# Block-causal attention and a gated MLP on one core: decode steps of the weights ranked below attention, constants by casting transfers, and two blocks of the weights' product side by side

## The chip, the cores and the metric

One core of one Trainium2 chip. The metric is the device time of one execution in microseconds. Engines are called as the profile calls them: PE (matrix), PEld (its weight loads), DVE (vector), ACT (scalar), POOL (GpSimd), SP (issues transfers only). Each engine takes its instructions in a fixed order, one after the other.

## The reference

```python
# batch 8, heads 8, seq 576, head_dim 64, blocks of 64; d_model 512, d_ff 1024
scores = q @ k.T / sqrt(64)                   # block-causal mask: block_i >= block_j
attn = exp(scores - rowmax); attn = attn / (sum(attn) + 1e-9)
x = concat_heads(attn @ v)                    # 4608 x 512
h = ((x @ w1) * (x @ w2)) @ w3
out = h @ w_out                               # float32
```

## The kernel before, in words

Heads are taken in pairs: a batch has four pairs, and there are 32 in all. `pair(n)` does the two heads j = 0 and 1 of pair n: score tiles s (a PSUM tile of up to 512 columns, two in turn), their exponentials pe, and the products x with the values; ahead of it, for the next pair, a bound on the row maxima from bf16 copies kb and qd (`shift_mask`: products mx, maxima m on DVE, a transposition mt, the negated result ms on ACT), which is written into a row of qk, the operand of the score matmuls (`shift`: for pair 0 by DVE from constants, for the others by POOL copies for pair 1 and small transfers qk<-ms that ACT issues). `prep_qk` rounds q and k into qk and subtracts to get the low parts. `norm` and `finish_x` divide by the row sums and split x into xh (ACT) and xl (POOL).

The MLP of one batch is the work beside the attention of the next. For batch 0 there is none yet, so its four pairs (the early stage, n < EARLY) run beside the preparation of the weights instead:

- The weights come as 64-bit numbers in 40 units of 0.5 MB, and `load_w` decodes one unit: a transfer wraw (five buffers); on ACT `wy` (the high word scaled, three buffers) and `top` (one byte of `wbits`, two of these buffers in turn); on POOL `low` (another byte of `wbits`); on DVE a combine of the two. Eight units are w_out (`wo`), sixteen w3, eight each w1 and w2. Those of w1 and w2 are then split (`load_rows`): a cast to w1h or w2h on DVE and a subtraction to w1l or w2l on POOL.
- `gen_prod` multiplies w3 by w_out on PE into W, eight blocks of eight matmuls, so that the MLP needs one product less. A block is copied out as wh and wl.

The order on PE is the order in which the code is written, for which EARLY_PLAN has one letter for each step of a pair's two heads: S a score tile, M a step of the next pair's maxima, B and A the preparations of q and k (own second head, next pair), V the products with v, Q loads the pair after next, N and T take and normalize x, C decodes one or two units (`weights`), W does two matmuls of W (`prod`). On the other engines the scheduler orders the instructions by rank and by when it expects their inputs; rank is the order of the code unless it is shifted. Each engine then waits in that order.

After pair 3 the rest of W is computed, the early buffers are given up, and the late stage begins, with attention of one batch beside the MLP of the one before.

Of the kernel before, what the change touches and what calls it, by code (L numbers as in the profile page):

```python
# [8 lines left out]
F32 = mybir.dt.float32  # L9
F32R = mybir.dt.float32r  # L10
BF16 = mybir.dt.bfloat16
I32 = mybir.dt.int32
# [36 lines left out]
)  # L49

EARLY_PLAN = (
# [8 lines left out]
)  # L60

DELAY = 3

# [4 lines left out]
def block_causal_attention__then__gated_mlp_kernel(ctx, tc, qkv, consts, ident_in, w1, w2, w3t, wout, out_t):  # L68
# [37 lines left out]
        raw_of[n] = t  # L106

    load(0)
    for t, tag in enumerate(("tr", "x32")):
        cst = work.tile([P, S], F32, tag=tag, name=f"cst{t}")  # L110
        nc.sync.dma_start(out=cst[0:D], in_=consts[:, t * S : (t + 1) * S])
        for j in range(2):
            nc.gpsimd.tensor_copy(qk[j][oth[j], 3 * t, :], cst[0:D])
    nc.sync.dma_start(out=both, in_=ident_in)
    nc.gpsimd.memset(qd, 0.0)

    tl = {}

    def open_early(pool):
        tl["early"] = pool  # L120
        tl["wo"] = pool.tile([P, NF, DM], F32, name="wo")
        tl["bits"] = [pool.tile([P, 512], I32, name=f"wbits{u}") for u in range(2)]
        tl["unit"] = 0
        for t in tl["bits"]:
            nc.gpsimd.memset(t, 0)

    def open_late():
        pool = ctx.enter_context(tc.tile_pool(name="late", bufs=1, reuse_waits="tile"))
# [7 lines left out]
        tl["gl"] = pool.tile([P, NF, HALF], F32R, name="gl")  # L136

    def load_w(dst, src):
        t = tl["early"].tile([P, 1024], I32, tag="wraw", name="wraw", bufs=5)
        y = tl["early"].tile([P, 512], F32, tag="wy", name="wy", bufs=3)  # L140
        bits = tl["bits"][tl["unit"] % 2]
        tl["unit"] += 1
        nc.sync.dma_start(out=t, in_=src)
        high = t.rearrange("p (c two) -> p c two", two=2)[:, :, 1]
        byte = t.bitcast(U8).rearrange("p (c e) -> p c e", e=8)
        if dst is None:
            dst = y
        low = bits.bitcast(U8).rearrange("p (c e) -> p c e", e=4)[:, :, 0]
        top = bits.bitcast(F8).rearrange("p (c e) -> p c e", e=4)[:, :, 3]
        nc.scalar.mul(out=y, in_=high.bitcast(F32), mul=2.0**-112)  # L150
        nc.scalar.activation(out=top, in_=byte[:, :, 7], func=AF.Copy, bias=127.5 * 2.0**-60, scale=-(2.0**-60), saturate=False)  # L151
        nc.gpsimd.tensor_scalar(out=low, in0=byte[:, :, 3], scalar1=1.0 / 32, scalar2=-31.0 / 64, op0=ALU.mult, op1=ALU.add)  # L152
        nc.vector.scalar_tensor_tensor(out=dst.bitcast(I32), in0=y.bitcast(I32), scalar=3, in1=bits, op0=ALU.logical_shift_left, op1=ALU.bitwise_or)
        return y
# [65 lines left out]
    def prep_qk(n, j):  # L220
        rqk = raw_of[n][:, 0 : 2 * S].rearrange("p (t s) -> p t s", t=2)
        o, x = own[j], oth[j]
        if j == 1:
            shift(n, 1)
        cast(n, qk[j][o, 0:2], rqk[o], CAST[0])
        yield
        if n == 0:
            copy = nc.gpsimd.tensor_copy if j else nc.scalar.copy
            copy(qk[j][x, 1, :], rqk[o, 1, :])
            copy(qk[j][x, 2, :], rqk[o, 0, :])  # L230
        else:
            queue(n).dma_start(out=qk[j][x, 1, :].bitcast(F32), in_=qk[j][o, 1, :].bitcast(F32))
            queue(n).dma_start(out=qk[j][x, 2, :].bitcast(F32), in_=qk[j][o, 0, :].bitcast(F32))
        yield
        (nc.gpsimd if "late" in tl or n * j else nc.vector).tensor_tensor(out=qk[j][o, 2:4], in0=rqk[o], in1=qk[j][o, 0:2], op=ALU.subtract)  # L235
        yield

    def prep_v(n, j):
        rv = raw_of[n][:, 2 * S :].rearrange("p (j c d) -> p j c d", j=2, c=5)[:, j]
        if n < EARLY:  # L240
            if n == 0:
                tl["ve", j] = tl["early"].tile([P, 5, P], F32, name=f"ve{j}")
                nc.gpsimd.memset(tl["ve", j][:, :, oth[j]], 1.0)
            nc.scalar.copy(tl["ve", j][:, :, own[j]], rv)
            return
        v = tl["vs"][j]
        cast(n, v[:, :, own[j]], rv, CAST[3])
        nc.gpsimd.tensor_tensor(out=v[:, :, oth[j]], in0=rv, in1=v[:, :, own[j]], op=ALU.subtract)
# [125 lines left out]
    def gen_w(wp):  # L374
        def rows(u):
            for k in range(2 * u, 2 * u + 2):
                load_w(tl["wo"][:, k, :], wout[k])

        def w3(m):
            assert done[0] >= m - 1  # L380
            t3_of[m] = wp.tile([P, NF, P], F32, tag="w3", name="w3", bufs=2)
            for h in range(2):
                load_w(t3_of[m][:, 4 * h : 4 * h + 4, :].rearrange("p k f -> p (k f)"), w3t[2 * m + h])

        def split(dst_h, dst_l, src):
            g = load_rows(dst_h, dst_l, src)
            return lambda _: next(g)

        one, two = split(w1h, w1l, w1), split(w2h, w2l, w2)
        for u in range(4):  # L390
            rows(u)
            yield
        m, rest = 0, [one] * 4 + [two] * 4
        while m < NF or rest:
            if m < NF and done[0] >= m - 1 and (m < 2 or len(rest) <= 9 - m or not rest):
                w3(m)
                m += 1
            else:
                rest.pop(0)(None)
            yield  # L400

    def gen_prod():
        wo = tl["wo"]
        for m in range(NF):
            acc = ps_m.tile([P, 512], F32, tag="psm", name=f"w{m}")
            for k in range(NF):
                nc.tensor.matmul(acc, t3_of[m][:, k, :], wo[:, k, :], start=(k == 0), stop=(k == NF - 1))  # L407
                if k % 2 and k < NF - 1:
                    yield
            nc.scalar.copy(wh[:, m, :], acc)  # L410
            nc.vector.tensor_tensor(out=wl[:, m, :], in0=acc, in1=wh[:, m, :], op=ALU.subtract)
            done[0] += 1
            yield

    def gen_moe(b):
        mp, gh, gl = tl["late"], tl["gh"], tl["gl"]
# [51 lines left out]
    def pair(n):  # L468
# [9 lines left out]
        for j in range(2):  # L478
            xps = ps_x.tile([P, 1024], F32, tag="psx", name=f"x{n}_{j}")
            p_early = wp.tile([P, 1600], F32, tag="pe", name=f"pe{n}_{j}") if early else None  # L480
            tiles = s_tiles(n, j, p_early)
            pvs = (pv_early if early else pv)(n, j, xps, p_early)
            delay = DELAY if n == NPAIR and j == 0 else 0
            for step in (EARLY_PLAN[n] if early else PLAN)[j].split():
                if step in "CW":
                    fill(weights if step == "C" else prod, 1)
                    continue
                with tc.high_priority(offset=0) if early else nullcontext():
                    if step == "S":
                        fill(tiles, 1)  # L490
                    elif step == "F":
                        if delay:
                            delay -= 1
                        else:
                            fill(mlp, 1)
                    elif step == "M":
                        fill(masks, 1)
                    elif step == "A":
                        fill(next_qk, 1)
                    elif step == "B":  # L500
                        fill(own_qk, 1)
                    elif step in "UV":
                        fill(pvs, 1)
                    elif step == "R":
                        sums(n, j, part)
                    elif step == "N" and early:
                        take_early(n, j, xps, x32, rr)
                    elif step == "N":
                        take(n, j, xps, x32)
                    elif step == "T":  # L510
                        if not early:
                            total(n, part, rr)
                        norm(n, x32, rr)
                        finish_x(n, x32)
                    elif step == "Q" and not last:
                        if n + 1 != NPAIR:
                            prep_v(n + 1, j)
                        if j == 1 and n + 2 < NN:
                            load(n + 2)
# [69 lines left out]
```

## Time and profile before

| | |
|---|---|
| median of 3 runs | 980.52 us (980.49 to 980.68) |
| the profiled execution | 982.55 us |
| its span, first to last instruction | 980.6 us |
| busy share of PE, DVE, ACT, POOL | 96%, 71%, 57%, 64% |
| mean granted clock of PE | 0.993 |

The profile lists for each engine when an instruction began, how long it took, and what ended the idle time before it. `[3.81 <-DMA qk<-ms]` behind a row is 3.81 us of idle time of that engine, ended by the landing of that transfer; rows that follow each other are merged, with their count behind an x. PE is the engine to watch: where it is idle, something else sets the pace. Buffer numbers are left out of names.

### The profile page before, as it was taken

The numbers are of one execution on the slowest core, as the hardware profiler recorded it, in microseconds if no ns is written. First come the engines' busy times: TensorE is split into PE (matmuls) and PEld (weight loads), VectorE is DVE, ScalarE is ACT, GpSimd is POOL, SyncE is SP. The second block draws the span as 40 slices with busy tenths as digits, with TensorE's granted clock in tenths as the row PEclk, the third lists the DMA queues.
The fourth block names the chain that finished last, engine by engine and source line by source line (L and its number), as shares of the span: only waits on it lengthen the run. The fifth ranks groups of instructions, "written<-read, shape, count | busy, mean of one in ns | idle before, by whom it ended". The sixth has DMA issues, their size and how long they took to land.

```text
span 980.6 us, 18312 instructions
## 1 busy us (share of the span) xinstructions
PE 941.6 (96%) x6594; PEld 879.1 (90%) x6624; DVE 692.4 (71%) x1230; ACT 557.3 (57%) x1451; POOL 629.6 (64%) x605
## 2 busy tenths in 40 slices
PE   3788989999999999999999999999999999999998
PEld 1444449999999999999999999999999999999998
DVE  6776857777777778878777777788787877774100
ACT  6776635656556665566565556655656555553221
POOL 6786737767676767677676767676776767673211
PEclk9999989999999999999999999999999999999999
DMA  8967502222222221222222221211222222100000
GB/s 294 304 198 221 163 19 62 63 75 63 87 63 75 63 87 41 66 69 65 73 66 83 64 80 57 88 54 53 69 72 66 69 81 63 50 13 25 7 19 25
DMA packets 31303, 79.81 MB, mean 81 GB/s; under 512 B 5356, under 2 KB 13676, under 8 KB 31212
## 3 DMA queue, kind: packets, MB, share of 16 engines
q1 hardware_dynamic: 29788, 76.26, 25.4%
q10 hardware_dynamic: 1424, 2.38, 1.0%
q8 instruction: 52, 0.85, 0.4%
q14 instruction: 39, 0.32, 0.1%
HBM read 50.76 MB, written 9.44 MB: 61 GB/s over the span
## 4 chain that ended last, share of the span: by engine, by line
PE 88%; ACT 3%; DVE 3%; POOL 3%; issue 2%; DMA 1%; ACTq 0%; SPq 0%; POOLq 0%; DVEq 0%
PE ab L426 42%; PE o L442 21%; PE s L265 9%; PE x L320 9%; PE mx L192 3%; PE w L407 2%; POOL wbits L152 1%; ACT wbits L151 1%; DMA wraw<-in_w 1%; ACT wy L150 1%; POOL w2l L162 1%; PE x L304 1%; DVE m L196 1%; ACT pe L273 1%; DVE qk L166 0%
## 5 line engine op out<-in xcount | busy, mean ns | idle before, releaser
L286 POOL TENSOR_TENSOR rsum<-rsum,p 128x448 f32<-128x448 f32 x224 | 186.1, 831 | 87.1 <-ACT p L280 76.8
L435 POOL TENSOR_TENSOR gl<-g,gh 128x288 fp32r<-128x288 f32 x128 | 114.5, 895 | 121.5 <-ACT gh L434 121.5
L283 DVE TENSOR_TENSOR pl<-p,ph 128x448 fp32r<-128x448 f32 x168 | 149.1, 901 | 60.1 <-ACT ph L281 59.2
L265 PE MATMUL s<-qk 128*128 128x288 f32 (+4 forms) x768 | 157.3, 314 | 16.3 <-ACT pe L273 10.8
L235 POOL TENSOR_TENSOR qk<-raw,qk 64x1152 fp32r<-64x1152 f32 x58 | 154.9, 2670 | 9.1 <-issue 6.1
L426 PE MATMUL ab<-xh,w2h 128*128 128x288 f32 x512 | 153.8, 300 | 0.0
L442 PE MATMUL o<-gh,wh 128*128 128x288 f32 x512 | 153.6, 300 | 0.0
L426 PE MATMUL ab<-xh,w1h 128*128 128x288 f32 x512 | 151.1, 295 | 0.0
L426 PE MATMUL ab<-xl,w2h 128*128 128x288 f32 x512 | 151.0, 295 | 0.0
L426 PE MATMUL ab<-xl,w1h 128*128 128x288 f32 x512 | 151.0, 295 | 0.0
L426 PE MATMUL ab<-xh,w1l 128*128 128x288 f32 x512 | 151.0, 295 | 0.0
L442 PE MATMUL o<-gh,wl 128*128 128x288 f32 x512 | 150.9, 295 | 0.0
L426 PE MATMUL ab<-xh,w2l 128*128 128x288 f32 x512 | 150.9, 295 | 0.0
L442 PE MATMUL o<-gl,wh 128*128 128x288 f32 x512 | 150.8, 295 | 0.0
L265 PEld LDWEIGHTS s<-qk 128*128 128x128 f32 (+1 forms) x768 | 116.9, 183 | 28.5 <-ACT pe L273 16.1
L434 ACT CAST gh<-g 128x288 fp32r<-128x288 f32 x128 | 55.4, 433 | 142.8 <-DVE g L433 142.7
L281 ACT ACTIVATE ph<-s 128x288 fp32r<-128x288 f32 x336 | 131.4, 393 | 0.0
L196 DVE TENSOR_REDUCE m<-mx 128x1 f32<-128x64 f32 (+3 forms) x320 | 128.3, 446 | 3.0 <-PE mx L192 0.8
L280 ACT ACTIVATE p<-s 128x448 f32<-128x448 f32 x224 | 85.5, 382 | 51.5 <-PE s L265 50.7
L283 DVE TENSOR_TENSOR pl<-rsum,ph 128x288 fp32r<-128x288 f32 x112 | 75.7, 677 | 49.2 <-ACT ph L281 45.4
L320 PE MATMUL x<-ph,vs 128*128 128x128 f32 x336 | 110.4, 329 | 0.0
L433 DVE TENSOR_TENSOR g<-ab,a 128x288 f32<-128x288 f32 x128 | 56.5, 441 | 69.5 <-PE ab L426 68.6
(76 smaller groups left out, 2182.4 us busy)
## 6 DMA issues: line engine op xcount, KB each, us to landing
raw<-in_qkv SPq DMA_DIRECT2D x31, 896.0 KB
qk<-qk SPq DMA_DIRECT2D x108, 144.0 KB
out_t<-o SPq DMA_DIRECT2D x64, 144.0 KB
wraw<-in_w3t SPq DMA_DIRECT2D x16, 512.0 KB
wraw<-in_w SPq DMA_DIRECT2D x16, 512.0 KB
wraw<-in_wout SPq DMA_DIRECT2D x8, 512.0 KB
qk<-qk ACTq DMA_DIRECT2D x16, 144.0 KB
qk<-ms SPq DMA_DIRECT2D x54, 2.2 KB
```

Source lines behind the costliest of these rows:

```text
L196: nc.vector.reduce_max(m[:, col : col + 1], sc, axis=AX.X)
L235: (nc.gpsimd if "late" in tl or n * j else nc.vector).tensor_tensor(out=qk[j][o, 2:4], in0=rqk[o], in1=qk[j][o, 0:2], op=ALU.subtract)
L265: nc.tensor.matmul(t[ks, at : at + q1 - q0], qk[j][:, k, kr], qk[j][:, q, q0:q1], start=(s == 0), stop=(s == 1))
L280: nc.scalar.activation(p32, t[ks, at : at + w], AF.Exp, scale=SCALE)
L281: nc.scalar.activation(ph[ks, o : o + w], t[ks, at : at + w], AF.Exp, scale=SCALE)
L283: nc.vector.tensor_tensor(out=low, in0=p32, in1=ph[ks, o : o + w], op=ALU.subtract)
L286: nc.gpsimd.tensor_tensor(out=r, in0=r, in1=p32, op=ALU.add)
L320: nc.tensor.matmul(xps[:, to : to + w], v[:, c, :], pr[:, a : a + w], start=(u < 2 and s == 0), stop=(u in (0, len(PV) - 1) and s == len(p ...
L426: nc.tensor.matmul(t[:, 0:HALF], l[:, c, fs], r, start=(c == 0 and s == 0), stop=(c == NC - 1 and s == 2))
L433: nc.vector.tensor_tensor(out=g32, in0=acc[1][:, 0:HALF], in1=a32, op=ALU.mult)
L435: nc.gpsimd.tensor_tensor(out=gl[:, f, :], in0=g32, in1=gh[:, f, :], op=ALU.subtract)
L442: nc.tensor.matmul(t[:, 0:HALF], l[:, f, es], r[:, f, :], start=(f == 0 and s == 0), stop=(f == NF - 1 and s == 2))
```

## The change

Six edits, all of the early stage.

1. Ranks: the steps C rank as if they stood 400 places later in the code. Before, attention steps had a shift of 0, decode steps none. The order of PE stays that of the code.
2. Constants: two transfers issued by POOL write them, cast, into qk; before, SP loaded them into two tiles and POOL cast them in four copies. The memsets at the start move from POOL to DVE.
3. `top` of the first twelve units moves from ACT to POOL (a comparison and a product that give the same byte).
4. Pair 0's two subtractions in `prep_qk` move from DVE to POOL.
5. Blocks 0 and 1 of W run side by side, one matmul of each in turn, so the order of the weights is w3's first two blocks, then w_out, then the rest. w3 gets three buffers instead of two, wraw four instead of five. W's steps C and W are placed anew in EARLY_PLAN.
6. A block of w3 may be decoded two blocks ahead of the product instead of one.

```diff
-    ("B B C M S S W B M S S M W C S M W V V M V V V Q N",
-     "M S S A C W S M S A W C S W V V A M V V V Q N T W W"),
+    ("B B C M S S W B M S S W M W C S M W V V M V V V Q N",
+     "M S S A C W S M S A C S W V V A M V W V V Q N T W W W W W"),
...
+LATER = 400
...
-    for t, tag in enumerate(("tr", "x32")):
-        cst = work.tile([P, S], F32, tag=tag, name=f"cst{t}")
-        nc.sync.dma_start(out=cst[0:D], in_=consts[:, t * S : (t + 1) * S])
-        for j in range(2):
-            nc.gpsimd.tensor_copy(qk[j][oth[j], 3 * t, :], cst[0:D])
+    for j in range(2):
+        nc.gpsimd.dma_start(out=qk[j][oth[j], 0:4:3, :], in_=consts.rearrange("p (t s) -> p t s", t=2))
     nc.sync.dma_start(out=both, in_=ident_in)
-    nc.gpsimd.memset(qd, 0.0)
+    nc.vector.memset(qd, 0.0)
...
-        t = tl["early"].tile([P, 1024], I32, tag="wraw", name="wraw", bufs=5)
+        t = tl["early"].tile([P, 1024], I32, tag="wraw", name="wraw", bufs=4)
...
-        nc.scalar.activation(out=top, in_=byte[:, :, 7], func=AF.Copy, bias=127.5 * 2.0**-60, scale=-(2.0**-60), saturate=False)
+        if tl["unit"] <= 12:
+            top = bits.bitcast(U8).rearrange("p (c e) -> p c e", e=4)[:, :, 3]
+            nc.gpsimd.tensor_scalar(out=top, in0=byte[:, :, 7], scalar1=128.0, scalar2=128.0, op0=ALU.is_ge, op1=ALU.mult)
+        else:
+            nc.scalar.activation(out=top, in_=byte[:, :, 7], func=AF.Copy, bias=127.5 * 2.0**-60, scale=-(2.0**-60), saturate=False)
...
-        (nc.gpsimd if "late" in tl or n * j else nc.vector).tensor_tensor(out=qk[j][o, 2:4], in0=rqk[o], in1=qk[j][o, 0:2], op=ALU.subtract)
+        (nc.gpsimd if "late" in tl or n == 0 or j else nc.vector).tensor_tensor(out=qk[j][o, 2:4], in0=rqk[o], in1=qk[j][o, 0:2], op=ALU.subtract)
...
-            assert done[0] >= m - 1
-            t3_of[m] = wp.tile([P, NF, P], F32, tag="w3", name="w3", bufs=2)
+            assert done[0] >= m - 2
+            t3_of[m] = wp.tile([P, NF, P], F32, tag="w3", name="w3", bufs=3)
...
+        for m in range(2):
+            w3(m)
+            yield
         for u in range(4):
             rows(u)
             yield
...
-            if m < NF and done[0] >= m - 1 and (m < 2 or len(rest) <= 9 - m or not rest):
+            if m < NF and done[0] >= m - 2:
...
+        acc = [ps_m.tile([P, 512], F32, tag="psm", name=f"w{m}") for m in range(2)]
+        for k in range(NF):
+            for m in range(2):
+                part(acc[m], m, k)
+            if k == NF - 1:
+                for m in range(2):
+                    out(acc[m], m)
             yield
...
                 if step in "CW":
-                    fill(weights if step == "C" else prod, 1)
+                    with tc.high_priority(offset=-LATER) if step == "C" else nullcontext():
+                        fill(weights if step == "C" else prod, 1)
                     continue
-                with tc.high_priority(offset=0) if early else nullcontext():
+                with nullcontext():
```

How this moves instructions is seen at three places. Numbers behind names tell tiles apart; they differ between the two kernels, and lines L are those of each kernel's own code (POOL's L152 is `low` before, `top` after; after, `low` is L155).

POOL between the shift copy of pair 1's second head and pair 0's product x, before:

```order
L216 COPY qk_87<-qk_87 9x576
L152 TENSOR_SCALAR wbits_109<-wraw 128x512
L235 TENSOR_TENSOR qk_87<-raw_188,qk_87 64x1152
L152 TENSOR_SCALAR wbits_110<-wraw 128x512
L358 TENSOR_TENSOR x_0_190<-x_0_190,rb_372 128x576
```

and after (six rows of three more units, which read like those ahead, are left out at the mark):

```order
L219 COPY qk_87<-qk_87 9x576
L152 TENSOR_SCALAR wbits_104<-wraw 128x512
L155 TENSOR_SCALAR wbits_104<-wraw 128x512
L238 TENSOR_TENSOR qk_87<-raw_184,qk_87 64x1152
L152 TENSOR_SCALAR wbits_103<-wraw 128x512
L155 TENSOR_SCALAR wbits_103<-wraw 128x512
...
L155 TENSOR_SCALAR wbits_103<-wraw 128x512
L361 TENSOR_TENSOR x_0_186<-x_0_186,rb_372 128x576
```

Two wbits steps became eleven (the one before x belongs to the thirteenth unit, whose `top` is on ACT again).

ACT at the same time, from pair 0's xh to pair 1's first exponentials, before:

```order
L367 CAST xh_0_375<-x_0_190 128x288
L367 CAST xh_1_379<-x_0_190 128x288
L151 ACTIVATE wbits_109<-wraw 128x512
L150 ACTIVATE wy<-wraw 128x512
L151 ACTIVATE wbits_110<-wraw 128x512
L166 CAST qd<-raw_365 64x9x64
L273 ACTIVATE pe_0_391<-s_0_423 128x288
L273 ACTIVATE pe_0_391<-s_0_419 128x288
```

and after:

```order
L370 CAST xh_0_375<-x_0_186 128x288
L370 CAST xh_1_379<-x_0_186 128x288
L276 ACTIVATE pe_0_386<-s_0_396 128x288
L276 ACTIVATE pe_0_386<-s_0_400 128x288
L149 ACTIVATE wy<-wraw 128x512 x2
```

The decode steps and the cast qd went from between xh and the exponentials; xh still stands ahead of them.

ACT ahead of the second head's first exponentials of pair 2, before:

```order
L273 ACTIVATE pe_0_634<-s_0_707 64x64
L151 ACTIVATE wbits_109<-wraw 128x512
L151 ACTIVATE wbits_110<-wraw 128x512
L150 ACTIVATE wy<-wraw 128x512 x2
L232 DMA qk_86<-qk_86 64x576
L233 DMA qk_86<-qk_86 64x576
L151 ACTIVATE wbits_109<-wraw 128x512
L244 COPY ve_154<-raw_606 128x5x64
L150 ACTIVATE wy<-wraw 128x512
L273 ACTIVATE pe_1_738<-s_1_744 128x288
```

and after:

```order
L276 ACTIVATE pe_0_605<-s_0_680 64x64
L154 ACTIVATE wbits_103<-wraw 128x512
L149 ACTIVATE wy<-wraw 128x512
L154 ACTIVATE wbits_104<-wraw 128x512
...
L149 ACTIVATE wy<-wraw 128x512
L247 COPY ve_148<-raw_584 128x5x64
L154 ACTIVATE wbits_103<-wraw 128x512
L349 COPY x_2_602<-x_0_604 64x576
L276 ACTIVATE pe_1_731<-s_1_737 128x288
```

Six decode steps stood between the two heads' exponentials, and nine stand there now (some left out here).

From the first `ab` matmul, the first exponentials ph and the first output transfer on, every engine has the same rows as before.

More of the change, by code (lines that the diff above doesn't have):

```diff
@@ L124, in open_early @@
         for t in tl["bits"]:
-            nc.gpsimd.memset(t, 0)
+            nc.vector.memset(t, 0)
     def open_late():
@@ L242, in prep_v @@
                 tl["ve", j] = tl["early"].tile([P, 5, P], F32, name=f"ve{j}")
-                nc.gpsimd.memset(tl["ve", j][:, :, oth[j]], 1.0)
+                nc.vector.memset(tl["ve", j][:, :, oth[j]], 1.0)
             nc.scalar.copy(tl["ve", j][:, :, own[j]], rv)
@@ L392, in gen_w @@
             yield
-        m, rest = 0, [one] * 4 + [two] * 4
+        m, rest = 2, [one] * 4 + [two] * 4
         while m < NF or rest:
-            if m < NF and done[0] >= m - 1 and (m < 2 or len(rest) <= 9 - m or not rest):
+            if m < NF and done[0] >= m - 2:
                 w3(m)
@@ L398, in gen_w @@
             else:
-                rest.pop(0)(None)
+                what = rest.pop(0)
+                what(None)
             yield
@@ L403, in gen_prod, with part, out @@
         wo = tl["wo"]
[L404 to L409, printed above, removed]
+        def part(acc, m, k):
+            nc.tensor.matmul(acc, t3_of[m][:, k, :], wo[:, k, :], start=(k == 0), stop=(k == NF - 1))
+        def out(acc, m):
             nc.scalar.copy(wh[:, m, :], acc)
@@ L412, in gen_prod @@
             done[0] += 1
-            yield
+        acc = [ps_m.tile([P, 512], F32, tag="psm", name=f"w{m}") for m in range(2)]
[5 more added lines that the diff above has]
+                    out(acc[m], m)
+            yield
+        for m in range(2, NF):
+            acc = ps_m.tile([P, 512], F32, tag="psm", name=f"w{m}")
+            for k in range(NF):
+                part(acc, m, k)
+                if k == NF - 1:
+                    out(acc, m)
+                if k % 2:
+                    yield
     def gen_moe(b):
```

12 rows, old and new, of the table EARLY_PLAN are left out of this document.

## The prediction

> **What bounds the kernel now.** I read the page's busy shares and its 40 slices first, then busy time by stage, then the PE timeline of the slices that are not full.
>
> ```profile
> PE 941.6 (96%) x6594; PEld 879.1 (90%) x6624; DVE 692.4 (71%) x1230; ACT 557.3 (57%) x1451; POOL 629.6 (64%) x605
> PE   3788989999999999999999999999999999999998
> PEclk9999989999999999999999999999999999999999
> ```
>
> PE is full from slice 7 on (24.5 us each, so from about 150 us). All instructions from the first `ab` product on stand in the same order in both kernels on every engine, so the change can only move the moment at which PE becomes full. The next table splits the time before it at the first score matmul of pairs 0, 1 (after its shift row), 2 and 3, at the end of pair 3's x, and at the end of the last product W. Columns: span, then busy us and count of PE, PEld, DVE, ACT, POOL, then the granted clock, DMA share and GB/s.
>
> ```profile
> 13.93:43.60 29.67, 18.08 (x70) 10.54 (x70) 19.84 (x34) 21.90 (x45) 19.24 (x17) 1.00 0.92 301
> 43.60:74.97 31.37, 28.03 (x93) 14.46 (x95) 24.46 (x38) 23.22 (x45) 26.27 (x20) 0.95 0.68 207
> 74.97:107.18 32.21, 28.18 (x96) 15.41 (x96) 21.80 (x35) 22.26 (x45) 19.89 (x18) 0.95 0.69 207
> 107.18:138.39 31.21, 25.13 (x85) 13.78 (x84) 23.48 (x34) 17.14 (x34) 20.47 (x16) 0.89 0.29 92
> 138.39:148.40 10.01, 10.01 (x26) 4.51 (x25) 3.44 (x6) 1.98 (x4) 1.58 (x2) 1.00 0.00 0
> ```
>
> No engine is full here except PE in the last row. PE idles 11.6, 3.3, 4.0 and 6.1 us in the four pairs, and runs below full clock behind its longer waits: (1-0.95) x 28.18 + (1-0.89) x 25.13 = 4.2 us in pairs 2 and 3 together. What it waits for:
>
> ```profile
> 21.36 0.61 PE L192 MATMUL mx<-kb,qd 128*128 128x512 bf16 x1 [4.79 <-ACT qd L166]
> 32.32 0.55 PE L265 MATMUL s<-qk 128*128 128x192 f32 x4 [0.94 <-ACT pe L273]
> 43.60 0.63 PE L265 MATMUL s<-qk 128*128 128x288 f32 x3 [3.81 <-DMA qk<-ms]
> 47.25 1.58 PE L265 MATMUL s<-qk 128*128 128x448 f32 x4 [0.44 <-ACT qd L166]
> 87.98 1.88 PE L407 MATMUL w<-wo,w 128*128 128x512 f32 x4
> 92.85 1.11 PE L265 MATMUL s<-qk 128*128 128x448 f32 x2 [3.00 <-ACT pe L273]
> 94.59 2.66 PE L407 MATMUL w<-wo,w 128*128 128x512 f32 x4
> 127.49 1.12 PE L265 MATMUL s<-qk 128*128 128x448 f32 x2 [3.65 <-ACT pe L273]
> 138.39 10.57 PE L407 MATMUL w<-wo,w 128*128 128x512 f32 x24
> ```
>
> (Of a product's matmul there are two records: x24 is 12 matmuls, 0.88 us each. The same four records take 2.66 us behind a 3.00 us wait and 1.88 otherwise.) Behind the waits stand decode steps that ACT had to pass first:
>
> ```profile
> 18.85 0.64 ACT L166 CAST kb<-raw 128x576 bf16<-128x576 f32 x1
> 19.40 0.67 ACT L166 CAST qd<-raw 64x576 bf16<-64x576 f32 x1
> 42.58 0.76 ACT L367 CAST xh<-x 128x288 fp32r<-128x288 f32 x2 [3.31 <-POOL x L358]
> 45.75 0.71 ACT L273 ACTIVATE pe<-s 128x288 f32<-128x288 f32 x2
> 91.83 0.67 ACT L150 ACTIVATE wy<-wraw 128x512 f32<-128x512 f32 x1 [1.65 <-POOL w2l L162]
> 92.39 0.70 ACT L273 ACTIVATE pe<-s 128x288 f32<-128x288 f32 x2
> 125.86 0.67 ACT L150 ACTIVATE wy<-wraw 128x512 f32<-128x512 f32 x1 [2.56 <-POOL w2l L162]
> 127.06 0.66 ACT L273 ACTIVATE pe<-s 128x288 f32<-128x288 f32 x2
> ```
>
> The exponentials at 92.39 and 127.06 were not late by themselves: a decode step ahead of them on ACT waited until POOL gave back its buffer. At 42.58 the split of x waits for POOL's product, with pair 1's exponentials queued behind it.
>
> **The change part by part.** The start first.
>
> ```profile
> 0.00:10.00 10.00, 1.01 (x2) 0.28 (x3) 5.42 (x5) 6.42 (x10) 7.26 (x13) 1.00 0.83 279
> 10.00:20.00 10.00, 3.90 (x13) 1.76 (x12) 7.65 (x17) 6.26 (x13) 5.82 (x8) 1.00 0.87 332
> 6.51 3.09 DVE L235 TENSOR_TENSOR qk<-raw,qk 64x1152 fp32r<-64x1152 f32 x2
> 9.63 4.01 DVE L196 TENSOR_REDUCE m<-mx 128x1 f32<-128x512 f32 x10
> 11.76 0.68 ACT L150 ACTIVATE wy<-wraw 128x512 f32<-128x512 f32 x1
> 15.48 1.09 PE L265 MATMUL s<-qk 128*128 128x288 f32 x3 [0.97 <-DVE qk L213]
> ```
>
> Pair 0's two subtractions leave DVE (3.09 us), so the maxima start at 6.5 instead of 9.63. That does not come through whole: the negated maxima stand behind the third `wy` on ACT, whose weights landed by 11.76 and now land about 1 us later, since the constants are read twice (0.3 MB more at 0.3 MB/us). Shift and scores follow at about 13.5 instead of 15.48. Then kb and qd of pair 1: 4.6 MB are ahead of or in raw 1 by the sizes in the page's last part (four transfers of w3t where four of wout stood, the same bytes), which at 279 and 332 GB/s is 15.5 us; kb 0.64, one `wy` about 0.65, two qd 1.34 give 18.2 instead of 21.36. Pair 0 runs 3.2 us earlier, and its last score matmul ends at 29.0 instead of 32.87 if half of its small waits also go.
>
> The memsets go to DVE, whose first work waits for a transfer: nothing, unless they outlast it. The constants need not be there before about 12.8; POOL's own issue of a transfer is not in this trace, the nearest row being the 4.6 us of the four casts that it replaces, so between 4.6 saved and as much lost, of which I take nothing because neither end reaches 12.8. One weight buffer less costs nothing while POOL takes longer for a unit (0.52 MB in 2.2 us, 240 GB/s) than the transfers at 301 GB/s.
>
> What POOL gets is the dear part.
>
> ```profile
> L152 POOL TENSOR_SCALAR wbits<-wraw 128x512 uint8<-128x512 uint8 x14 | 14.2, 1012 | 10.4 <-DVE wo L153 6.2 <-DMA wraw<-in_w 2.4 <-DMA wraw<-in_w3t 1.1
> L152 POOL TENSOR_SCALAR wbits<-wraw x40: 762/825/1832, 11.7 to 123.6; 128x512 uint8<-128x512 uint8 x40
> 31.55 1.73 POOL L152 TENSOR_SCALAR wbits<-wraw 128x512 uint8<-128x512 uint8 x1 [1.15 <-DMA wraw<-in_w3t]
> 31.29 1.34 DVE L235 TENSOR_TENSOR qk<-raw,qk 64x1152 fp32r<-64x1152 f32 x1
> L113 POOL CAST qk<-cst 64x576 fp32r<-64x576 f32 x4 | 4.6, 1147 | 1.9 <-DMA cst<-in_consts 1.7
> L235 POOL TENSOR_TENSOR qk<-raw,qk 64x1152 fp32r<-64x1152 f32 x4 | 10.8, 2704 | 7.1 <-issue 6.1 <-DVE qk L166 0.8
> 33.35 1.00 POOL L216 CAST qk<-qk 9x576 fp32r<-9x576 f32 x1
> 41.15 1.40 POOL L358 TENSOR_TENSOR x<-x,rb 128x576 f32<-128x576 f32 x1
> L162 POOL TENSOR_TENSOR w1l<-wy,w1h 128x512 fp32r<-128x512 f32 x8 | 13.7, 1729 | 0.4
> ```
>
> Twelve `top` operations move from ACT. On POOL this operation (a comparison and a product) is not in the trace; the nearest row is `low`, the same shape and types: 0.76 to 1.83 us, mean 1.01 in the first 45 us, which I take, with 0.08 to the next: 1.09. Between the second shift copy and pair 0's product x stand now eleven such steps and one subtraction (three rows before). The copy waits for the scores' end: 29.0 + 1.0 = 30.0; 11 x 1.09 + 2.70 = 14.7 gives 44.7; x 1.40, the two xh 0.76, the first exponential about 0.4: 47.3, where pair 1's third score tile had begun at 47.25. So the 3.2 us are lost again in POOL's queue: **0 us**. Its ends: at the median 0.825, 2.0 us earlier; at 1.83, 9 us later and more, since the fourteen steps, the subtraction and the copy ahead (from about 10 us, with a wait for DVE's first combine near 15) end at about 30 too and have no slack either.
>
> Pair 1 has 2.9 us of idle behind 47.25 (3.34 less 0.44). Its exponentials no longer stand behind steps that wait for POOL, which has two w1 subtractions there instead of six: I take 0.5 left, a gain of 2.4. At the hand-over to pair 2 only two matmuls of W, not six, and some x stand between the transposition of the maxima and the next scores, 3 to 4 us against a shift that needs 4.5 to 5: a new wait of 1.5. The two accumulators side by side hold both buffers until ACT and DVE have copied them out; two score and three x matmuls stand between, about as long as the copies, so I add nothing. **0.9 us** gained.
>
> Pairs 2 and 3 hold 10.1 us of idle and 4.2 of slow clock. Matmuls of W stand more evenly now: ten instead of six in pair 2's first half, eight instead of six in pair 3's, each 0.88 us of work while ACT catches up; the last ten, not twelve, are left for the end. Against it POOL has fourteen of its sixteen 1.7 us subtractions from pair 2 on (ten before), all four blocks of w2 in pair 3, and ACT still has `wy` steps ahead of the second half's exponentials that need a buffer from them. So neither all nor nothing: half, **7.1 us**. The end of w2 is covered by the last ten matmuls, 8.8 us; without that cover POOL's last two, 3.4 us, would show.
>
> Sum: 0 + 0.9 + 7.1 = 8.0 us. The profiled execution (span 980.6, itself 982.55) lies 2.0 above the median of the runs, 980.52; I take the gain off the median: **972.5 us**.
>
> One page speaks to the clock term: the Trainium skill, "TensorE: Matmul & The Clock Gate" (What's actually happening), has the clock halved after an idle window of about 3.4 us. The row above shows slow matmuls behind 3.00 us already, so this trace does not quite agree; by the page, waits all cut below 3.4 us would give back the whole 4.2, and the sum would be 970.4.
>
> **The rivals.** *The waits go almost wholly.* POOL at its median (2.0), the 13.0 us of idle in pairs 1 to 3 down to 1.5 (11.5), the clock back (4.2), 0.5 at the hand-over: 17.2 us, 963.3. For it: no engine but PE was above 85% of any pair. Against: POOL's added 17 us (twelve steps at 1.0, two subtractions at 2.7) lie in the same stage.
>
> *Nothing is gained.* The same buffer waits stay in pairs 2 and 3, because the four subtractions pushed there (6.8 us of POOL) undo the better rank; what pair 1 gains remains: 979.6. For it: both long waits came from POOL, not from rank; against: POOL is idle for 12.3 of 32.2 and 10.7 of 31.2 us there.
>
> *Slower: POOL becomes the bound early.* One mechanism: its 25 wbits steps between the first weights and pair 0's x go at the dear price. The step at 31.55 took 1.73 beside the subtraction on DVE. Each 0.1 us more is 2.5 us later at pair 1; the 8.0 are used up at a mean of 1.33 us, and at 1.5 the end is 25 x 0.49 - 8.0 = 4.2 later: 984.7. Against: half of the forty took 0.825 us or less. The Trainium skill, "GPSIMD Engine Reference" (Specifications), states that GpSimd shares its SBUF interfaces with VectorE and contends with instructions that have two SBUF inputs; the pair of rows agrees. By that rule every unit's combine on DVE would slow the steps beside it, and with all 25 at 1.83 the time would be 993.
>
> **How the numbers follow.** Forecast 0.50, waits gone 0.22, nothing gained 0.12, slower 0.16. A change of 0.2% (2 us) is about what a measurement of this kernel can tell from none. Faster: 0.50 + 0.22 = 0.72; same 0.12; slower 0.16. The range reaches from a little past the second case to the measurable edge of the third, with half of the slower case left out at the top (0.1) and a few hundredths below: 962 to 982. The forecast alone: 967 to 977, from 2 us either way at pair 1 and a quarter to three quarters of the 14.3.
>
> **What would show it.** Right: pair 1's third score tile near 47 with ACT's xh still waiting for POOL's x; PE's idle in pairs 2 and 3 near 5 us and clock above 0.95; W's last eight matmuls starting near 131 and PE full from about 140. Wrong: `top` on POOL away from 1.0 us; exponentials waiting 3 us or more behind `wy`; the first scores later than 15.5 for want of the constants; PE idle between W's end and `ab` for w2.

## The result: slower, and the profile after

The changed kernel takes 1003.57 us (median of 5 runs, 1002.53 to 1005.25) against 980.52 for the kernel before on the same chip: a ratio of 1.0239, 95% interval 1.0218 to 1.026. The forecast was 972.5, the range 962 to 982.

Busy shares and slices on the page of the changed kernel:

```profile
PE 946.1 (95%) x6624; PEld 882.2 (88%) x6624; DVE 694.0 (69%) x1233; ACT 550.9 (55%) x1439; POOL 656.0 (66%) x612
PE   2758889999999999999999999999999999999998
PEclk9969999999999999999999999999999999999999
```

PE's third slice (50 to 75 us) is 5 tenths where it was 8, at a granted clock of 0.6. POOL has 26 us more (656.0 against 629.6), ACT 6 less. The next table cuts the early part at PE's first score matmul behind pair 0's shift row, the shift row and the third score tile of pair 1, the third score tiles of pairs 2 and 3, and the first `ab` (columns as in the prediction), first after:

```profile
16.19:48.29 32.10, 19.36 (x67) 11.66 (x68) 14.63 (x25) 14.41 (x30) 30.13 (x19) 1.00 0.59 177
48.29:64.94 16.65, 4.26 (x9) 1.75 (x9) 4.65 (x8) 1.86 (x5) 15.43 (x11) 0.61 0.45 152
64.94:97.17 32.23, 28.26 (x92) 15.53 (x92) 20.60 (x33) 22.45 (x45) 17.57 (x17) 0.88 0.67 197
97.17:131.64 34.47, 29.82 (x101) 15.91 (x100) 25.19 (x38) 23.03 (x45) 23.86 (x20) 0.95 0.70 201
131.64:168.99 37.35, 32.53 (x105) 17.27 (x104) 29.57 (x43) 19.14 (x39) 26.56 (x20) 0.91 0.30 94
```

and of the kernel before with the same marks (the first two rows of after are one here):

```profile
15.48:47.25 31.77, 20.71 (x75) 11.49 (x76) 22.11 (x37) 25.23 (x51) 22.17 (x20) 0.96 0.90 289
47.25:77.65 30.40, 27.50 (x95) 14.63 (x97) 21.42 (x35) 21.61 (x44) 25.47 (x19) 0.98 0.70 219
77.65:110.43 32.78, 28.44 (x95) 15.38 (x96) 24.38 (x39) 22.66 (x47) 19.51 (x18) 0.95 0.65 192
110.43:149.32 38.89, 33.12 (x103) 17.61 (x103) 24.34 (x37) 17.06 (x35) 20.30 (x16) 0.91 0.19 56
```

POOL (the fifth busy column) is now busy for 45.6 of the first 48.75 us, ACT for 16.3; before it was 22.2 and 25.2 of 31.8. This stage alone grew by 17.0 us. The rest, pair 1's third tile to `ab`, takes 104.05 us where it took 102.07. Together with a first score 0.7 us later that is the 19.7 us by which `ab` starts later (168.99 against 149.32); the spans differ by 20.1. (The medians differ by 23.05, because the profiled execution of the kernel before lies 2.0 us above its median and that of the changed kernel 1.0 below.) PE's waits in the timeline after:

```profile
16.19 1.09 PE L268 MATMUL s<-qk 128*128 128x288 f32 x3 [4.62 <-DVE qk L216]
48.29 0.78 PE L268 MATMUL s<-qk 128*128 128x288 f32 x3 [4.23 <-DMA qk<-ms]
64.94 1.65 PE L268 MATMUL s<-qk 128*128 128x448 f32 x4 [12.39 <-ACT pe L276]
93.56 1.09 PE L268 MATMUL s<-qk 128*128 128x288 f32 x3 [3.50 <-DMA qk<-ms]
116.23 0.68 PE L268 MATMUL s<-qk 128*128 128x448 f32 x2 [4.65 <-ACT pe L276]
148.04 1.11 PE L268 MATMUL s<-qk 128*128 128x448 f32 x2 [3.73 <-ACT pe L276]
168.99 0.29 PE L448 MATMUL ab<-xh,w1h 128*128 128x288 f32 x1
```

The 12.39 us wait was 0.44 before. Behind it, POOL's groups up to the product x (mean ns of one stands after the busy time):

```profile
L152 POOL TENSOR_SCALAR wbits<-wraw 128x512 uint8<-128x512 uint8 x12 | 29.1, 2425 | 4.3 <-DMA wraw<-in_w3t 2.8 <-POOL qk L219 0.7
L155 POOL TENSOR_SCALAR wbits<-wraw 128x512 uint8<-128x512 uint8 x13 | 10.4, 800 | 0.9
L238 POOL TENSOR_TENSOR qk<-raw,qk 64x1152 fp32r<-64x1152 f32 x3 | 9.4, 3140 | 0.9 <-DVE qk L169 0.7
```

L152 is the `top` step, a comparison and a product: 2.43 us. L155 is `low`, a product and a sum over the same shape and types: 0.80. The forecast had priced the first by the second. How this reaches PE is in the timeline of DVE, ACT and POOL:

```profile
50.85 0.69 DVE L156 SCALAR_TENSOR_TENSOR wo<-wy,wbits 128x512 int32<-128x512 int32 x1 [5.52 <-POOL wbits L155]
54.35 0.69 DVE L156 SCALAR_TENSOR_TENSOR wo<-wy,wbits 128x512 int32<-128x512 int32 x1 [2.81 <-POOL wbits L155]
57.86 0.69 DVE L156 SCALAR_TENSOR_TENSOR wo<-wy,wbits 128x512 int32<-128x512 int32 x1 [2.81 <-POOL wbits L155]
58.58 0.78 DVE L347 STREAM_TRANSPOSE tr<-x 64x576 f32<-64x576 f32 x1
59.39 0.63 ACT L349 COPY x<-x 64x576 f32<-64x576 f32 x1 [12.13 <-DVE tr L347]
54.40 2.59 POOL L152 TENSOR_SCALAR wbits<-wraw 128x512 uint8<-128x512 uint8 x1
62.26 1.40 POOL L361 TENSOR_TENSOR x<-x,rb 128x576 f32<-128x576 f32 x1
63.69 0.76 ACT L370 CAST xh<-x 128x288 fp32r<-128x288 f32 x2 [3.66 <-POOL x L361]
64.47 0.71 ACT L276 ACTIVATE pe<-s 128x288 f32<-128x288 f32 x2
```

DVE's combines wait for POOL one after the other, and the transposition tr of pair 0's sums stands behind them in DVE's order. ACT's copy of x waits 12.13 us for tr, then ACT waits for POOL's x, which has the same steps ahead of it; pair 1's exponentials stand behind both.

### The profile page after: what moved, and what is told of

The parts are those of the page before. It is cut to its first block, busy times and chain, and to the rows that moved or that the text cites. A ratio compares the mean times of both kernels' runs of the same rounds, so it can differ in the third digit from the quotient of the medians.

```text
span 1000.7 us, 18349 instructions
## 1 busy us (share of the span) xinstructions
PE 946.1 (95%) x6624; PEld 882.2 (88%) x6624; DVE 694.0 (69%) x1233; ACT 550.9 (55%) x1439; POOL 656.0 (66%) x612
## 4 chain that ended last, share of the span: by engine, by line
PE 87%; POOL 5%; issue 2%; DMA 2%; DVE 2%; ACT 2%; SPq 0%; ACTq 0%; POOLq 0%; DVEq 0%
PE ab L448 41%; PE o L464 21%; PE s L268 9%; PE x L323 8%; PE mx L195 4%; PE w L413 2%; POOL wbits L152 2%; POOL wbits L155 1%; DMA wraw<-in_w3t 1%; PE x L307 1%; POOL w1l L165 1%; DMA qk<-ms 1%; POOL w2l L165 0%; ACT pe L276 0%; PE tot L340 0%
## 5 line engine op out<-in xcount | busy, mean ns | idle before, releaser
L238 POOL TENSOR_TENSOR qk<-raw,qk 64x1152 fp32r<-64x1152 f32 x60 | 162.4, 2707 | 5.2 <-DVE qk L169 2.9
```

The source lines that it names most:

```text
L238: (nc.gpsimd if "late" in tl or n == 0 or j else nc.vector).tensor_tensor(out=qk[j][o, 2:4], in0=rqk[o], in1=qk[j][o, 0:2], op=ALU.subtract)
```

## The experiments

Times are given with the ratio to the kernel before on the same chip and its 95% interval. "Edit" numbers: 1 the rank, 2 the constants by casting transfers and the memsets on DVE, 3 `top` of twelve units on POOL, 4 pair 0's subtractions on POOL, 5 and 6 the new order of the weights' product. The theory after the result: the 23 us come from edit 3, by the price of the step. The rivals: the other work put on POOL, or a path by the product x alone.

**`top` of all units back on ACT (edit 3 undone).**

```diff
-        if tl["unit"] <= 12:
-            ...
-            nc.gpsimd.tensor_scalar(out=top, ..., op0=ALU.is_ge, op1=ALU.mult)
-        else:
-            nc.scalar.activation(out=top, ...)
+        nc.scalar.activation(out=top, ...)
```

> The changed kernel with `top` of all 40 units on ACT again (edit 3 alone undone). Theory A (the price of the comparison): on POOL it takes 2.1 to 2.6 us instead of the 1.0 forecast, and twelve of them push pair 0's x from 41 to 62 us; without them x comes back to about 43, pair 1's third score tile to about 47, and the time to 984 to 987 (the later waits of pairs 2 and 3, 2 us worse than before, stay). Theory B (the other edits cost it: ranks, casting transfers, plan): the time stays above 1000.

Measured: 980.08 us, ratio 0.9983 (0.9971 to 0.9995). 4 us below the lower end of what was expected. Edit 3 carries the whole loss and a little more; the rest of the change is worth 0.2%, not the 0.8% forecast.

**The same bit by a cheaper operation on POOL.** A product and a sum into float16, whose sign is the bit:

```diff
-            top = bits.bitcast(U8)...[:, :, 3]
-            nc.gpsimd.tensor_scalar(out=top, ..., scalar1=128.0, scalar2=128.0, op0=ALU.is_ge, op1=ALU.mult)
+            top = bits.bitcast(mybir.dt.float16)...[:, :, 1]
+            nc.gpsimd.tensor_scalar(out=top, ..., scalar1=-(2.0**-60), scalar2=127.5 * 2.0**-60, op0=ALU.mult, op1=ALU.add)
```

> The changed kernel with `top` of the first twelve units still on POOL and at the same place, but as a product and a sum into a 16-bit float whose sign is the byte's top bit, no comparison. Theory A: it is the operation; this one costs about what `low` costs, 0.8 to 1.0 us, so 12 x 1.5 us come off POOL and the time is 983 to 988. Rival C (the place: any twelve steps more on POOL beside DVE's combines are slow and queue ahead of x): steps stay near 2 us or x stays later than 55, time above 995.

Measured: 991.11 us, ratio 1.0101 (1.0079 to 1.0123), 3 us above the upper end of what was expected. Its POOL groups up to x, and PE's wait:

```profile
L152 POOL TENSOR_SCALAR wbits<-wraw 128x512 f16<-128x512 uint8 x12 | 13.0, 1082 | 5.2 <-DVE w L156 2.5 <-DMA wraw<-in_w3t 1.3 <-DVE wo L156 0.7
L155 POOL TENSOR_SCALAR wbits<-wraw 128x512 uint8<-128x512 uint8 x13 | 11.1, 850 | 0.9
```

```profile
50.98 1.65 PE L268 MATMUL s<-qk 128*128 128x448 f32 x4 [7.20 <-ACT pe L276]
```

With the step at 1.08 instead of 2.43 us the time falls by 12.5 us, about half of edit 3's loss; x starts at 48.30, so the rival of the place (x later than 55) falls. But (13.0 + 11.1) / 25 = 0.96 us a step is below the 1.01 that the forecast used, and the kernel is still slower than before. So the price is not the only error: see below.

**The comparison without its product** (`op0=ALU.is_ge` alone; the sign bits of the weights come out wrong).

> The changed kernel with `top` on POOL as the comparison alone, without the product by 128 (the sign byte is then wrong, all else is as in the changed kernel). If the comparison itself is dear: still 2.1 us or more a step and 1000 us or more. If it is the second operation behind it: 0.8 to 1.2 a step and 985 to 992.

One run: 999.8 us. The group:

```profile
L152 POOL TENSOR_SCALAR wbits<-wraw 128x512 uint8<-128x512 uint8 x12 | 23.7, 1979 | 4.2 <-DMA wraw<-in_w3t 2.2 <-POOL qk L219 0.7 <-DVE w L156 0.6
```

The comparison alone takes 1.98 us where it takes 2.43 with the product behind it. Both figures lie just under what was expected of a dear comparison (2.1 us, 1000 us) and far from what was expected of a dear second operation.

**Edit 3 alone, on the kernel before.**

> The kernel before with edit 3 alone (`top` of the first twelve units as a comparison on POOL). Theory A: about 12 x 2.5 = 30 us more on POOL ahead of pair 0's x, of which some 12 us fill its idle time: x at about 59 instead of 41, time 995 to 1000. Theory B: 980 to 984, since ACT is freed of 9 us.

Measured: 1002.38 us, ratio 1.0207 (1.0187 to 1.0227), 2 us above what was expected. The step takes 2.09 us or more here too (median 2.59), x starts at 60.65. Without edit 4's load on POOL the loss is as large: the rival of the other work on POOL falls.

**The product x of pairs 0 and 1 on DVE instead of POOL.**

```diff
-        (nc.gpsimd if n < 2 else nc.vector).tensor_tensor(out=x32, ...)
+        nc.vector.tensor_tensor(out=x32, ...)
```

> The changed kernel with the product x of pairs 0 and 1 on DVE instead of POOL, `top` still compared on POOL. If the loss goes by the chain POOL's queue, x, xh on ACT, pair 1's exponentials, it is cut here although POOL is as slow as before: pair 1's third score tile near 52 instead of 65, time 989 to 993. If POOL's slowness acts mainly by the weights (w_out decoded too late for W), PE waits there instead and the time stays above 999.

Measured: 1001.73 us, ratio 1.0208 (1.0185 to 1.0231), almost 9 us above what was expected. The timeline says why:

```profile
57.77 0.69 DVE L156 SCALAR_TENSOR_TENSOR wo<-wy,wbits 128x512 int32<-128x512 int32 x1 [2.81 <-POOL wbits L155]
59.30 0.64 ACT L349 COPY x<-x 64x576 f32<-64x576 f32 x1 [12.12 <-DVE tr L347]
63.09 1.65 PE L268 MATMUL s<-qk 128*128 128x448 f32 x4 [9.87 <-ACT pe L276]
```

POOL's queue ahead of x was one of two legs, nearly equally late. The other, combine and tr on DVE, stayed, and PE gained 1.85 us at this tile (63.09 against 64.94), of which nothing is left at `ab` (169.74 against 168.99). The time is that of the other branch, above 999, but not for its reason: PE's long wait here is for the exponentials as before, not for the product's weights.

The next runs ask where the gain of the rest went.

**Edit 2's transfers undone as well** (on top of `top` on ACT: the constants by SP and four casts on POOL).

> `top` on ACT throughout, and the constants again by two SP transfers and four casts on POOL (edits 3 and 2's transfers undone; memsets stay on DVE). Theory: the casting transfers made the first weights land 2 us later, and the negated maxima wait behind them on ACT; with the old path the first `wy` starts near 9 instead of 10.9, the scores with the shift near 14.5 to 15.5 instead of 16.4, time 1 to 2 us under e1_top_act. Rival: POOL's casts (4.6 us) delay the subtraction for the first scores by as much, time equal or up to 2 us above.

Measured: 980.24 us, ratio 0.9986 (0.9964 to 1.0008): not to be told from the 980.08 with them. A miss; the first scores did come earlier, 13.33 instead of 16.40, and the lead was lost later. The time is the rival's, but its cause, later first scores, was not seen.

**The rank undone** (`LATER = 0`, `top` on ACT).

> `top` on ACT throughout, and the decode steps C at the rank of their place (edits 3 and 1 undone). Theory of the prediction (rank takes the exponentials out from behind the buffer waits, about half of 14 us): 985 to 988. Rival (both long waits come from POOL's buffers, not from rank): within 2 us of e1_top_act, 978 to 982.

Measured: 988.84 us, ratio 1.0077 (1.005 to 1.0104), 0.8 us above the upper end: the rank is worth about 9 us in this kernel.

**The rank alone, on the kernel before.**

```diff
+LATER = 400
-                    fill(weights if step == "C" else prod, 1)
+                    with tc.high_priority(offset=-LATER) if step == "C" else nullcontext():
+                        fill(weights if step == "C" else prod, 1)
-                with tc.high_priority(offset=0) if early else nullcontext():
+                with nullcontext():
```

> The kernel before with edit 1 alone (C ranked 400 places later). Theory of the prediction: 3 to 7 us faster than before. Rival (rank gains nothing by itself): 979 to 983; with w_out still decoded first and W's steps where they were, decode falls behind and it may even be slower.

Measured: 976.24 us, ratio 0.9943 (0.9922 to 0.9964), within the 3 to 7 us expected. Its stages from pair 1's third tile on:

```profile
51.37:80.34 28.97, 26.77 (x97) 14.37 (x96) 21.70 (x34) 17.58 (x37) 20.91 (x17) 1.00 0.61 195
80.34:110.39 30.05, 27.13 (x96) 14.23 (x96) 25.93 (x38) 21.91 (x46) 19.54 (x17) 1.00 0.77 226
110.39:142.98 32.59, 30.33 (x104) 15.73 (x103) 26.91 (x39) 19.25 (x39) 21.03 (x17) 1.00 0.27 83
```

```profile
42.80 6.46 PE L409 MATMUL w<-wo,w 128*128 128x512 f32 x8 [8.44 <-DVE w L155]
```

91.6 us where it was 102.1, at full clock: here is the gain forecast for pairs 1 to 3. Ahead of it a new wait of 8.44 us takes 4.1 back, because a product step in front of pair 1's scores now waits for a decode that was ranked down. While PE waits there the decode goes on, so a part of the gain behind it may be this head start and not the rank; the two were not separated. Net, `ab` is 6.3 us earlier.

**Rank and new order (edits 1, 5, 6); rank and start (edits 1, 2, 4); rank with the first product steps moved behind pair 1.**

> The kernel before with the rank (edit 1) and the new order of the weights' product (edits 5 and 6), without the casting transfers, the moved memsets, the top step on POOL and pair 0's subtractions on POOL. The rank alone measured 976.24 us, 5.6 us under the kernel before; with edits 2, 4, 5 and 6 added and top on ACT it was 980.08, 1.5 us under. Theory A, the 4 us are given back by edits 5 and 6 (the score waits for exponentials of 2.7 to 2.9 us in pairs 2 and 3 that the rank alone does not have): 979 to 981 us. Theory B, they are given back by edits 2 and 4 at the start (first scores behind a 4.6 us wait for the subtraction's neighbour, first weights 2 us later): 975 to 977 us.

> The kernel before with the rank (edit 1), the constants by casting transfers and memsets on DVE (edit 2), and pair 0's subtractions on POOL (edit 4); the old order of the weights' product, top on ACT. Theory A (edits 5 and 6 give the 4 us back): 975.5 to 977.5 us, as the rank alone. Theory B (edits 2 and 4 do): 979 to 981 us.

> The kernel before with the rank, and in the plan the two W steps at the end of pair 0 stand at the end of pair 1. With the rank alone TensorE waits 8.44 us at 42.80 us for the decoded block of the first W step, and stands in front of pair 1's scores there. Theory, that wait is what the rank leaves: the scores go in from about 38 us, and the time falls by 2 to 5 us under the rank alone, 971 to 974 us. Rival, pair 1's scores are no earlier (their operands or the exponentials wait for the same DVE and ACT queues) or the later W steps run into the same decode: 976 to 977 us.

Measured: 976.46 (ratio 0.9947, 0.9925 to 0.9968), 977.47 (0.995, 0.9935 to 0.9965) and 983.73 us (1.0012, 0.9996 to 1.0029). The first two are level with the rank alone: neither theory A nor B holds as it was put, for neither half of the change gives the 4 us back by itself. They go when the two halves meet; the next run asks whether it is edit 4 that does it. The third is a miss: pair 1's scores went in at 36.51, but the next product step then waited 5.42 us for the same decode, as the rival had it, and the scores behind it up to 4.31 for their exponentials. The time is almost 7 us above the rival's.

**Edits 1, 2, 5 and 6 (3 and 4 undone).**

```diff
-        (nc.gpsimd if "late" in tl or n == 0 or j else nc.vector).tensor_tensor(out=qk[j][o, 2:4], ...)
+        (nc.gpsimd if "late" in tl or n * j else nc.vector).tensor_tensor(out=qk[j][o, 2:4], ...)
```

> The changed kernel with the top step of all units on ACT and pair 0's two subtractions back on DVE (edits 3 and 4 undone; rank, casting transfers and the new order of the weights' product stay). Theory, with the new order it is edit 4 that costs the last 4 us: it makes pair 0 and pair 1 about 2 us earlier, and pair 2's shift row is then sent while the weights' transfers fill the queues and lands no earlier, behind which TensorE is slowed: 975.5 to 977.5 us, as with the rank and the new order alone (976.46). Rival, any two of the edits beside the rank and the order cost it (edit 2 makes the first weights late): 979 to 981 us, as with edits 2 and 4 (980.08).

Measured: 971.97 us, ratio 0.9909 (0.9892 to 0.9926): the fastest of all, and below both forecasts. With edit 4 it was 0.9983 (0.9971 to 0.9995). So the two subtractions, moved to save 3 us on DVE at the start, cost about 7 us here. Without the casting transfers they cost about 4 (0.9986 with edit 4, 0.9947 without, though there the memsets differ too). Against edits 1, 5 and 6 alone (0.9947, 0.9925 to 0.9968) edit 2, transfers and memsets together, gains here, by intervals that just touch; beside edit 4 its transfers made no difference. The stages:

```profile
16.04:40.15 24.11, 19.41 (x75) 11.64 (x76) 15.73 (x28) 16.54 (x35) 11.46 (x10) 1.00 0.68 227
40.15:69.52 29.37, 26.95 (x91) 13.88 (x92) 22.74 (x35) 22.88 (x47) 19.34 (x18) 0.96 0.79 252
69.52:104.08 34.56, 30.50 (x99) 16.29 (x100) 30.18 (x41) 25.47 (x50) 25.82 (x21) 0.94 0.73 220
104.08:138.35 34.27, 31.50 (x104) 16.82 (x103) 31.31 (x42) 20.63 (x42) 25.57 (x20) 0.95 0.38 122
```

The stage lengths of the runs side by side (us, read from PE's timeline with the same marks):

| kernel (edits) | first scores | to pair 1's third tile | to pair 2's | to pair 3's | to `ab` | `ab` at |
|---|---|---|---|---|---|---|
| before (none) | 15.48 | 31.77 | 30.40 | 32.78 | 38.89 | 149.32 |
| changed (1 to 6) | 16.19 | 48.75 | 32.23 | 34.47 | 37.35 | 168.99 |
| 3 | 15.92 | 51.07 | 31.19 | 32.39 | 38.43 | 169.00 |
| 1 to 6, `top` by float16 | 14.81 | 36.17 | 33.40 | 34.83 | 37.82 | 157.03 |
| 1, 2, 4, 5, 6 | 16.40 | 28.38 | 28.39 | 35.82 | 37.86 | 146.85 |
| 1, 4, 5, 6, memsets on DVE | 13.33 | 28.50 | 32.59 | 36.08 | 36.53 | 147.03 |
| 2, 4, 5, 6 | 17.37 | 32.17 | 31.54 | 34.34 | 39.43 | 154.85 |
| 1 | 15.79 | 35.58 | 28.97 | 30.05 | 32.59 | 142.98 |
| 1, later product steps | 15.38 | 30.82 | 38.52 | 30.71 | 35.14 | 150.57 |
| 1, 2, 4 | 16.74 | 35.07 | 28.99 | 30.05 | 33.85 | 144.70 |
| 1, 5, 6 | 15.83 | 27.37 | 28.89 | 34.78 | 35.58 | 142.45 |
| 1, 2, 5, 6 | 16.04 | 24.11 | 29.37 | 34.56 | 34.27 | 138.35 |

The new order takes 8 us off the first stage (27.37 against 35.58, no product step waits there) and gives about the same back in pairs 2 and 3 (4.7 and 3.0). Two more of the product's matmuls, 1.8 us, stand in pair 2's stage; the rest is more idle time and a lower clock than with the rank alone:

```profile
72.09:106.87 34.78, 30.14 (x100) 15.93 (x100) 27.93 (x40) 24.41 (x48) 25.70 (x21) 0.95 0.68 214
106.87:142.45 35.58, 31.84 (x103) 16.70 (x103) 29.87 (x42) 19.56 (x40) 27.16 (x20) 0.95 0.34 107
```

How edit 4 costs stays open. With the casting transfers (1, 2, 4, 5, 6 against the last row) the first scores start within 0.4 us, yet from there to pair 1's third tile it takes 4.3 us longer (ACT casts pair 1's kb at 19.77 instead of 17.63), and the last stage 3.6. Without them (1, 4, 5, 6 against 1, 5, 6) the first scores are 2.5 us earlier and the loss lies mostly elsewhere: 3.7 us up to pair 2's third tile and 1.3 up to pair 3's. No run shows one cause for both.

## Why the prediction was wrong, point by point

- **The step that failed: 12 `top` steps at 1.01 us, "0 us".** They took 2.43. With 13 `low` at 0.80 the mean of the 25 steps is 39.5 / 25 = 1.58 us, and by the prediction's own line 25 x (1.58 - 1.01) = 14.2 us. Pair 1's third tile was forecast at 47.3 and came at 64.94, 17.6 later. The price explains most; it was taken from a row of the same shape, but of another operation. Of the 17.6 us, 10.5 had arisen by the end of the second shift copy (40.47, forecast 30.0), behind the first fourteen steps, and 7.1 between it and x.
- **The rest of that term.** With the float16 form the mean was 0.96, and the tile still came at 50.98, 3.7 us late. Of this, 2.8 us were there at the end of the second shift copy (32.76 for 30.0): the first scores came at 14.81 instead of 13.5, and from 16.34 on POOL worked up to the copy without a pause. Behind it, the subtraction took 3.13 us instead of 2.70. The count also let x wait for POOL's own queue alone. In fact every combine on DVE waits for POOL and tr stands behind four of them; in the float16 kernel this leg was the later one, x waiting 0.45 us for it, and in the changed kernel it would have held PE to 63.09 by itself (the run with x on DVE).
- **The slower rival** named the place (POOL early, pair 1 late) and gave 984.7, or 993 with all 25 steps at 1.83. Its cause was another: it took the dear price from contention with DVE. The `top` step at 54.40 took 2.59 us while DVE, from 55.04 on, only waited for it, and `low` was dear nowhere up to x (mean 0.80). The Trainium skill, "GPSIMD Engine Reference" (Specifications), has GpSimd and VectorE contend for their shared SBUF interfaces; that is not what made this step dear here. Nor is 984.7 near: with the measured mean of 1.58 us the rival's line gives 986.8, and most of the rest is that the 8.0 us which it took as gained did not come (2.0 were lost) and that pair 1's third tile was another 3.4 us late. Its chance, 0.16, was too low: a queue with no slack and an operation without a row deserved more.
- **First scores at 13.5.** They came at 16.19 in the changed kernel and at 13.33 without the casting transfers. The prediction saw that the negated maxima stand behind the third `wy` on ACT, but allowed 1 us for its weights. ACT's rows after:

```profile
14.07 0.67 ACT L149 ACTIVATE wy<-wraw 128x512 f32<-128x512 f32 x1 [0.63 <-DMA wraw<-in_w3t]
14.76 0.27 ACT L205 ACTIVATE ms<-mt 9x128 fp32r<-9x128 f32 x1
```

  The third `wy` was 2.3 us later than before (14.07 against 11.76), and the negated maxima, whose input was on hand at 11.26, waited for it. The error moved the end by nothing that could be measured (980.24 us without the casting transfers, 980.08 with them).
- **Pairs 1 to 3, 8.0 us (0.9 + 7.1).** Right for the rank, as far as the head start of its decode is not the reason: alone it gains 10.5 us there, clock 1.00, longest wait 2.26. Wrong for the whole: 104.05 us after, 2.0 lost; 102.07 with `top` on ACT, nothing gained; 98.20 without edit 4 as well, 3.9 gained. The step that failed here is that the product's matmuls, spread more evenly, would leave half of the waits: PE's idle time from pair 1's third tile to `ab` (span less busy) was 13.0 us before and 13.4 after, 12.1 with edits 1, 5 and 6 and 9.3 with 1, 2, 5 and 6, where the rank alone left 7.4. Pair 2's stage grew from 32.78 to 34 to 36 us in every kernel with the new order, of which two more matmuls are 1.8. The argument against it in the prediction, POOL's subtractions pushed into pairs 2 and 3, fits better, though no run moved them alone. The waits there were still for exponentials behind `wy` steps that wait for POOL:

```profile
113.70 0.67 ACT L149 ACTIVATE wy<-wraw 128x512 f32<-128x512 f32 x1 [1.17 <-POOL w1l L165]
115.78 0.69 ACT L276 ACTIVATE pe<-s 128x288 f32<-128x288 f32 x2
```

- **Edit 4 at the start** was costed as 3.09 us saved on DVE; the work that it adds to POOL was named, but no term of the sum charged for it. With the new order it cost 4 to 7 us.
- **The forecast's time.** 972.5 is nearly that of edits 1, 2, 5 and 6 (971.97), but by another sum: 7.1 us from the start that was set to 0 (40.15 for 47.25) and 3.9 from the pairs set to 8.0. By PE's marks that is 11.0; the median fell by 9.4. That it agrees with the forecast is chance.

## What to carry to other kernels

An operation that the trace does not show has no price: a row of the same shape and types, but another operation, was off by a factor of 2.4, and where the receiving queue has no slack that price decides the answer (here 14.2 of 17.6 us), so it is worth one run by itself. When work moves to a queue, follow not only that queue but the engine that consumes its results in order: what stands behind the consumer waits as well. A bundle is judged by its parts: here four edits together gain 0.9%, two cost 3.3%, and the fastest kernel that was run is the bundle without those two.

## What the runs showed of the hardware

- On POOL, 128x512 of uint8 took 0.80 us for a product and a sum, 1.98 for a comparison, 2.43 for a comparison and a product, 1.08 for a product and a sum into float16 (means of the 12 or 13 steps up to pair 0's x; the first took 0.85 beside the float16 form). The three forms of `top` have two sizes each, about 0.5 us apart (1.65 and 2.1; 2.1 and 2.6; 0.76 and 1.2); what sets them was not tried.
- A small transfer landed later where the queues were fuller. Pair 2's shift row (two transfers of 2.2 KB) in the run with edits 1, 4, 5 and 6, and in that with 1, 5 and 6; the DMA share is the last column but one:

```profile
66.00:68.00 2.00, 0.42 (x2) 0.19 (x1) 1.93 (x4) 0.98 (x2) 1.74 (x2) 1.00 1.05 297
70.06 1.09 PE L267 MATMUL s<-qk 128*128 128x288 f32 x3 [3.63 <-DMA qk<-ms]
```

```profile
66.00:68.00 2.00, 2.00 (x9) 0.99 (x7) 1.58 (x2) 1.52 (x3) 1.30 (x2) 1.00 0.61 147
69.84 0.67 PE L267 MATMUL s<-qk 128*128 128x288 f32 x3 [1.48 <-DMA qk<-ms]
```

  The first of the two was issued from 65.00 in the first run and from 66.80 in the second, and yet the scores started 0.2 us later in the first. In the next 2 us the shares were 0.99 and 0.88. One profile of each; no run varied the transfers alone, so it is not shown that the load was the cause.
- Slow matmuls follow waits far shorter than 3 us, but not always. In the fastest kernel:

```profile
65.99 0.67 PE L264 MATMUL s<-qk 128*128 128x288 f32 x3 [1.39 <-DMA qk<-ms]
66.49 3.16 PE L409 MATMUL w<-wo,w 128*128 128x512 f32 x4
```

  and with edits 1, 5 and 6:

```profile
40.18 0.63 PE L267 MATMUL s<-qk 128*128 128x288 f32 x3 [1.62 <-DMA qk<-ms]
40.65 1.88 PE L412 MATMUL w<-wo,w 128*128 128x512 f32 x4
```

  The Trainium skill, "TensorE: Matmul & The Clock Gate" (What's actually happening), has an idle window of about 3.4 us that runs freely; a single wait of 1.39 us is less than half of it, so the window alone does not explain these rows.
